# Attention scores as plain float32 products instead of three products of high and low parts

## The chip, the cores and the metric

The kernel runs on one core of a Trainium2 chip. The metric is the device time of one execution in microseconds (us), median of three runs. The engines are named as the profile names them: PE (TensorE: matrix products; PEld its weight loads), DVE (VectorE), ACT (ScalarE), POOL (GpSimd) and SP (which issues most DMAs). Each works through its own queue in order, and they meet through semaphores.

## What is computed

A causal attention is followed by two mixture-of-experts layers. Only the attention is touched by the change:

```python
batch, n_heads, seq, head_dim = (4, 12, 448, 64)
scale = 1.0 / np.sqrt(q.shape[-1])
scores = scale * np.matmul(q, k.transpose(0, 1, 3, 2))
mask = np.triu(np.ones((seq, seq), dtype=bool), k=1)
scores = np.where(mask, -1000000000.0, scores)
scores = scores - np.max(scores, axis=-1, keepdims=True)
attn = np.exp(scores)
attn = attn / (np.sum(attn, axis=-1, keepdims=True) + 1e-09)
return np.matmul(attn, v).astype(np.float32)
```

Its output, 1792 tokens of 768 numbers, goes through a layer with 8 experts (two products with 768x1024 and 1024x768 weights per expert) and then through a second one of the same size.

## The kernel before

**Tiling.** The 48 heads are worked as 24 pairs. The two heads of a pair (e = 0, 1) lie in partitions 0 to 63 and 64 to 127 of one tile `r` that holds keys and queries, transposed, as 2x448 columns of float32. The 448 queries of a head are cut into four chunks of 112; chunk c needs the keys of chunks 0 to c only, 112(c+1) columns. A score tile `sc` is one PSUM bank (128x512 float32), and there are four of them: two chunks of two heads.

**Scores.** `qk(g, c)` makes the scores of pair g and chunk c for both heads. Queries and keys have each been split by `split_pair` into a high part `hi` (type float32r, which PE multiplies in one record) and a low part `lo`; the score is the sum of hi·hi, hi·lo and lo·hi (L423), the two heads alternating, and a last product per head adds the mask (L425, bfloat16, `identb` times `mask`, 1e30 above the diagonal; scores are negated, so the row's minimum is the maximum). `split_pair` runs on POOL two pairs ahead: it scales the queries in place (L386), copies to `hi` (L164, in `pcopy`) and subtracts for `lo` (L167, in `psub`). For the first two pairs it runs on DVE and ACT (L392 to L396).

**Around them.** Per pair and chunk, `rowmax` (L430, DVE) takes the row minimum from PSUM into `nm`, `expo` (L435, ACT) reads the same bank and writes `ex`, which frees the bank. `halves_hi` (ACT, L443) and `halves_lo` (DVE, L448, `al<-ex,ah`) split `ex` in two 16-bit parts that DMAs transpose; `last_chunk` transposes chunk 3 on PE (L457) and splits it (L460, L462). `values` multiplies with the values (L490, L494), `combine` normalises (L501 to L509), `route_t` and `route_l` (L518 to L531) prepare the routing of the first expert layer. `split_v` (POOL, L167, `r<-vr` and `r<-r`) splits the values.

**Order.** All queues are written out by hand in one loop over g (L800): pair g's scores, pair g-1's last chunk, pair g-2's values, pair g-3's routing. In PE's queue an iteration reads: chunks 0 and 1 of pair g; transposes; `values` of head 0; chunks 2 and 3 of pair g; transposes; `values` of head 1; `route_l`. Small routing steps on DVE are dealt out between the others by `tick`.

Of the kernel before, what the change touches and what calls it, by code (L numbers as in the profile page):

```python
# [9 lines left out]
F32 = mybir.dt.float32  # L10
F32R = mybir.dt.float32r
# [5 lines left out]
ALU = mybir.AluOpType  # L17
# [6 lines left out]
P = 128  # L24
B, H, S, HD = 4, 12, 448, 64
CP, NCH = 112, 4
NT, D, F, E = 1792, 768, 1024, 8
# [17 lines left out]
NAH = 2  # L45
NTH = 3
NTP = 2
PLACES = (0, 7, 2, 4, 6, 5, 3, 1)
AHEAD = 2
NONE = 2.0 * E * E + E  # L50
# [5 lines left out]
def attention_two_moe_kernel(  # L56
# [17 lines left out]
    vec, act, pool, pe = nc.vector, nc.scalar, nc.gpsimd, nc.tensor  # L74
# [15 lines left out]
    mask = const.tile([CP, 512], BF16, name="mask")  # L90
# [3 lines left out]
    zero8 = const.tile([P, E], F32, name="zero8")  # L94
    vec.memset(zero8, 0.0)
    st_v, st_x, st_q = ExitStack(), ExitStack(), ExitStack()
    right = lambda st, nm, bufs: st.enter_context(tc.tile_pool(name=nm, bufs=bufs, side="right", reuse_waits="tile"))
# [2 lines left out]
    av_p = right(st_v, "av_p", 1)  # L100
    xb_p = right(st_v, "xb_p", 2)
    at_p = right(st_x, "at_p", 1)
    ld_p = right(st_q, "ld_p", 4)
    raw = right(st_q, "raw", 1)
    ps_s = st_q.enter_context(tc.tile_pool(name="ps_s", bufs=4, space=PSUM, side="right", reuse_waits="tile"))

    his, los = ([raw.tile([P, 2 * S + P - CP], F32R, name=f"{nm}{i}") for i in range(3)] for nm in ("hi", "lo"))
    for t in his + los:
        for k in range(0, P - CP, E):
            vec.tensor_copy(t[:, 2 * S + k : 2 * S + k + E], zero8)  # L110
    identb = const.tile([CP, P], BF16, name="identb")
    vec.tensor_copy(identb, ident[:CP])
    iota_i = const.tile([P, JB * E], I32, name="iota_i")
# [49 lines left out]
    def pcopy(dst, src):  # L163
        pool.tensor_scalar(out=dst, in0=src, scalar1=1.0, scalar2=1.0, op0=ALU.mult, op1=ALU.mult)  # L164

    def psub(dst, a, b):
        pool.tensor_tensor(out=dst, in0=a, in1=b, op=ALU.subtract)  # L167
# [158 lines left out]
    tls = [av_p.tile([P, 2 * ND * CP + 16], F16, name=f"tl{i}") for i in range(NTH)]  # L326
    phs = [av_p.tile([CP, 2 * NCH * CP + 16], F16, name=f"ph{i}") for i in range(NTP)]
    pls = [av_p.tile([CP, 2 * NCH * CP + 16], F16, name=f"pl{i}") for i in range(NTP)]
    for t in ahs + als:
# [38 lines left out]

    NPR = B * H // 2
    PB = H // 2  # L370
    raws, spl, vrs, vss = {}, {}, {}, {}
    def load_pair(g):
        b, i = divmod(g, PB)
        r = ld_p.tile([P, 2, S], F32, tag="r", name=f"r{g}")
# [5 lines left out]
        vrs[g] = av_p.tile([CP, 2, NCH, HD], F32, tag="vr", name=f"vr{g}", bufs=6)  # L380
        nc.sync.dma_start(vrs[g], vh[b, :, 2 * i : 2 * i + 2])

    def split_pair(g, fast=False):
        r = raws.pop(g)
        if not fast:
            pool.tensor_scalar(out=r[:, 1], in0=r[:, 1], scalar1=-0.125, scalar2=1.0, op0=ALU.mult, op1=ALU.mult)  # L386
        hi, lo = his[g % 3], los[g % 3]
        spl[g] = hi[:, :S], lo[:, :S], hi[:, S:], lo[:, S:]
        r = r.rearrange("p k s -> p (k s)")
        hi, lo = hi[:, : 2 * S], lo[:, : 2 * S]  # L390
        if fast:
            vec.tensor_scalar(out=hi[:, S:], in0=r[:, S:], scalar1=-0.125, scalar2=1.0, op0=ALU.mult, op1=ALU.mult)  # L392
            act.copy(hi[:, :S], r[:, :S])
            vec.scalar_tensor_tensor(out=lo[:, S:], in0=r[:, S:], scalar=-0.125, in1=hi[:, S:].bitcast(F32),
                                     op0=ALU.mult, op1=ALU.subtract)
            vec.tensor_sub(lo[:, :S], r[:, :S], hi[:, :S].bitcast(F32))  # L396
        else:
            pcopy(hi, r)
            psub(lo, r, hi.bitcast(F32))

    def split_v(g):
        r0 = vrs.pop(g)
# [7 lines left out]
    boff = [0, 1, 3, 6]  # L410
    scs, nms, avs = {}, {}, {}

    def qk(g, c):

        kh, kl, qh, ql = spl[g]
        n = CP * (c + 1)
        cs = slice(c * CP, (c + 1) * CP)
        for e in range(2):
            scs[2 * g + e, c] = ps_s.tile([P, 512], F32, tag="sc", name=f"sc{2 * g + e}_{c}")
        for st, (a, b) in enumerate(((qh, kh), (qh, kl), (ql, kh))):  # L420
            for e in range(2):
                rs = slice(e * HD, (e + 1) * HD)
                pe.matmul(scs[2 * g + e, c][:, :n], lhsT=a[rs, c * CP : c * CP + P], rhs=b[rs, :n], start=(st == 0), stop=False)  # L423
        for e in range(2):
            pe.matmul(scs[2 * g + e, c][:, cs], lhsT=identb, rhs=mask[:, :CP], start=False, stop=True)  # L425

    def rowmax(h, c):
        if c == 0:
# [246 lines left out]
            load_v(g)  # L675
    load_consts()
    clear_meta()
    split_pair(0, True)
    xbs = {}
    routing = prep_en()  # L680
    for _ in range(8):
# [118 lines left out]
    for g in range(NPR + 3):  # L800
        t, v, r = g - 1, g - 2, g - 3
        if g + 4 < NPR:
            load_pair(g + 4)
        if g + 3 < NPR:
            load_v(g + 3)
        if r == 0:
            drain(routing)
            routing = None
            vec.tensor_scalar_mul(tau_h, tau_t, 0.5)
            vec.reciprocal(tau_r, tau_h)  # L810
            for b in range(B):
                vec.tensor_copy(mts[b][:, :, 3], mod_i[:, b * NCH : (b + 1) * NCH, 0])
        if 0 <= v < NPR and v % PB == 0:
            xbs[v // PB] = xb_p.tile([CP, NCH, D], F32, tag="xb", name=f"xb{v // PB}")
        late = [last_chunk(t, e) if 0 <= t < NPR else iter(()) for e in range(2)]
        if g < NPR:
            for c in range(2):
                qk(g, c)
        tick(True)
        if g < NPR:  # L820
            for c in range(2):
                both(rowmax, g, c)
                if g == c == 0:
                    both(expo, 0, 0, ticks=False)
                    split_pair(1, True)
            for c in range(g == 0, 2):
                both(expo, g, c, ticks=False)
        next(late[0], None)
        next(late[0], None)
        if 0 <= t < NPR:  # L830
            halves_lo(t, (0,))
        next(late[0], None)
        if 0 <= t < NPR:
            halves_lo(t, (1,))
        if g == NPR + 2:
            warm(ps_T, "T", WV)
        if 0 <= r < NPR:
            if r == NPR - 1:
                for c in range(NCH):
                    route_ss(B - 1, c, xbs[B - 1], 2)  # L840
                last_root = route_root(B - 1)
                next(last_root)
            route_t(r, xbs[r // PB])
            if r == NPR - 2:
                for c in range(NCH):
                    route_ss(B - 1, c, xbs[B - 1], 1)
        if g == NPR + 1:
            split_w(1, (4, 5), range(3))
            warm(ps_T, "T", WV)
        if 0 <= v < NPR:  # L850
            values(v, 0)
        if PB <= r < NPR and r % PB < NCH:
            b = r // PB - 1
            c = -1
            for c in ((0,), (1,), (2,), (3,))[r % PB] if b < B - 2 else ((0, 1), (2, 3), (), ())[r % PB]:
                store_x(b, c)
                route_ss(b, c, xbs[b])
            if c == NCH - 1:
                drain(routing or ())
                routing = route1(b)  # L860
        if g < NPR:
            for c in range(2, NCH):
                qk(g, c)
                both(rowmax, g, c)
        next(late[1], None)
        for c in range(2, NCH):
            if g < NPR:
                both(expo, g, c, ticks=False)
            next(late[1], None)
        if 0 <= v < NPR:  # L870
            values(v, 1)
        if 0 <= r < NPR:
            route_l(r)
        if 0 <= v < NPR:
            combine(v, xbs[v // PB])
        if g < NPR:
            halves_hi(g)
        if g + 2 < NPR:
            split_pair(g + 2)
        if g == 0:  # L880
            split_v(0)
        if g + 1 < NPR:
            split_v(g + 1)
        if LEAD <= g <= NPR:
            for c in range(g - LEAD, KD if g == NPR else g - LEAD + 1):
                load_lead(m1, 1, c)
        if g == NPR - 1:
            st_q.close()
            ps_h = left("ps_h", 2, space=PSUM)
            ps_T = left("ps_T", 2, space=PSUM)  # L890
            wh, w1l = left("wh", 1), ()
            w1h = [wh.tile([P, F], F32R, name=f"w1h{c}") for c in range(KD)]
            for k in range(2):
                pcopy(w1h[k], w1r[k])
        if g == NPR:
            split_w(1, (2, 3), ())
            st_x.close()
            wb = left("wb", 1)
            w1l = [wb.tile([P, F], F32R, name=f"w1l{c}") for c in range(KD)]
            w2r = [wb.tile([P, D], F32, name=f"w2r{f}") for f in range(KF)]  # L900
            m1.gather_early((0,), 2 * S)
            load_lead(m1, 2)
        if g == NPR + 2:
            split_w(1, (), range(3, KD))
    drain(routing)
    b = B - 1
# [630 lines left out]
```

## Time and profile before

| | us |
|---|---|
| median of three runs | 921.96 |
| the three runs | 918.61, 923.04, 921.96 |
| the profiled execution, its own time | 910.5 |
| span of its trace | 908.7 |

The profiled execution is a run of its own, 1.2% under the median of the three; between its span and its time lie 1.8 us. Times in the trace count from the span's start. Matmuls overlap, and the end of one is modelled; what one costs in a row of them is read from start to start.

### The profile page before, as it was taken

How to read it: one execution, taken by the hardware profiler on the slowest of the kernel's cores; microseconds unless marked ns; L12 is line 12 of the kernel's file. 1: busy time of each engine (PE TensorE's matmuls, PEld its weight loads, DVE VectorE, ACT ScalarE, POOL GpSimd, SP SyncE). 2: the span in 40 equal slices, each digit the busy share in tenths (PEclk: the TensorE clock that was granted, in tenths of full speed). 3: DMA queues.
4: the chain of work that ended last, by engine and by line, in shares of the span. 5: the costliest groups of instructions: out<-in, count | busy, mean ns of one | idle time of the engine just before them, and what ended most of it. 6: DMA issues, size and time to landing. Idle time of an engine off the chain costs nothing. (4 is left out here: it accounts for less than half of the span.)

```text
span 908.7 us, 21165 instructions
## 1 busy us (share of the span) xinstructions
PE 859.1 (95%) x7010; PEld 753.3 (83%) x7010; DVE 699.3 (77%) x1798; ACT 427.8 (47%) x779; POOL 478.0 (53%) x477
## 2 busy tenths in 40 slices
PE   4999999999789899999999999999999999999995
PEld 3877877877577899998898999888899898898984
DVE  7899999999785766787936884468886678976793
ACT  3676777767434664575525652245112133312323
POOL 7877577875255255454444564431653544544531
PEclk9999999999899999999999999999999999999998
DMA  6799996979717765578515662120281233511110
GB/s 193 161 154 171 203 181 159 210 172 218 241 53 254 278 257 176 203 282 296 193 38 183 201 231 97 53 76 6 57 332 39 67 88 133 185 48 54 54 38 16
DMA packets 114456, 137.46 MB, mean 151 GB/s; under 512 B 78382, under 2 KB 82788, under 8 KB 114289
## 3 DMA queue, kind: packets, MB, share of 16 engines
q1 hardware_dynamic: 101376, 108.76, 44.1%
q0 software_dynamic: 12912, 26.83, 9.4%
q8 instruction: 61, 1.00, 0.5%
q14 instruction: 107, 0.87, 0.3%
HBM read 101.48 MB, written 19.92 MB: 134 GB/s over the span
## 5 line engine op out<-in xcount | busy, mean ns | idle before, releaser
L765 POOL DMA_INDIRECT xg<-x,xi x128 | 137.7, 1076 | 98.3 <-DMA x<-yb,mg 50.8
L974 PE MATMUL h<-w1h,xh 128*128 128x512 f32 x408 | 165.0, 404 | 1.0 <-ACT xh L958 1.0
L976 PE MATMUL h<-w1h,xl 128*128 128x512 f32 x408 | 161.5, 396 | 1.0 <-DVE xl L959 1.0
L975 PE MATMUL h<-w1l,xh 128*128 128x512 f32 x408 | 161.3, 395 | 0.2 <-DVE w1l L715 0.2
L1039 PE MATMUL o<-w2h,hh 128*128 128x384 f32 x528 | 138.3, 343 | 0.2 <-ACT hh L988 0.2
L1039 PE MATMUL o<-w2h,hl 128*128 128x384 f32 x528 | 136.7, 340 | 0.9 <-DVE hl L989 0.9
L1039 PE MATMUL o<-w2l,hh 128*128 128x384 f32 x528 | 136.0, 339 | 0.1
L1016 DVE STREAM_TRANSPOSE hs<-h 32x256 f32<-32x256 f32 x240 | 107.0, 446 | 14.3 <-PE h L976 9.0
L435 ACT ACTIVATE ex<-sc,nm 112x112 f32<-112x112 f32 (+1 forms) x192 | 83.8, 503 | 62.2 <-DVE nm L430 60.9
L1039 PEld LDWEIGHTS o<-w2h,hl 128*128 128x128 f32 x528 | 96.4, 190 | 1.2 <-DVE hl L989 1.2
L1039 PEld LDWEIGHTS o<-w2l,hh 128*128 128x128 f32 x528 | 96.1, 189 | 0.7 <-DVEq L1330 0.4
L1039 PEld LDWEIGHTS o<-w2h,hh 128*128 128x128 f32 x528 | 94.8, 190 | 1.8 <-ACT hh L988 0.4
L976 PEld LDWEIGHTS h<-w1h,xl 128*128 128x128 f32 x408 | 77.3, 190 | 19.6 <-DVE xl L959 2.0
L1022 ACT ACTIVATE hh<-hs 128x512 fp32r<-128x512 f32 x30 | 18.4, 631 | 158.1 <-PE o L1039 88.6
L974 PEld LDWEIGHTS h<-w1h,xh 128*128 128x128 f32 x408 | 77.5, 190 | 16.6 <-ACT xh L958 1.1
L975 PEld LDWEIGHTS h<-w1l,xh 128*128 128x128 f32 x408 | 77.5, 190 | 16.2 <-DVE w1l L715 1.0
L715 DVE TENSOR_TENSOR w1l<-w1r,w1h 128x1024 fp32r<-128x1024 f32 x66 | 76.5, 1221 | 8.3 <-ACT w1h L713 7.5
L430 DVE TENSOR_REDUCE nm<-sc 112x1 f32<-112x112 f32 (+1 forms) x192 | 75.6, 439 | 6.1 <-PE sc L425 5.0
L715 DVE TENSOR_TENSOR w2l<-w2r,w2h 128x768 fp32r<-128x768 f32 x78 | 68.8, 953 | 8.2 <-ACT w2h L713 6.9
L713 ACT CAST w1h<-w1r 128x1024 fp32r<-128x1024 f32 x64 | 62.4, 1046 | 8.4 <-PE h L976 5.2
L947 DVE STREAM_TRANSPOSE xr<-xg 128x768 f32<-128x768 f32 x31 | 50.4, 1625 | 18.8 <-DMA xg<-x,xi 14.9
L713 ACT CAST w2h<-w2r 128x768 fp32r<-128x768 f32 x78 | 58.5, 849 | 0.6 <-ACTq L1421 0.6
(327 smaller groups left out, 1932.7 us busy)
## 6 DMA issues: line engine op xcount, KB each, us to landing
w1r<-in_w1a SPq DMA_DIRECT2D x48, 512.0 KB, 6.8
w2r<-in_w2a SPq DMA_DIRECT2D x64, 384.0 KB, 6.2
r<-in_kqP SPq DMA_DIRECT2D x24, 448.0 KB, 4.3
w1r<-in_w1b SPq DMA_DIRECT2D x18, 512.0 KB, 6.5
w2r<-in_w2b SPq DMA_DIRECT2D x24, 384.0 KB, 6.4
vr<-in_vh SPq DMA_DIRECT2D x24, 224.0 KB, 4.4
x<-xb SPq DMA_DIRECT2D x16, 336.0 KB, 4.3
xg<-x,xi POOLq DMA_INDIRECT x128, 3.3
```

The costliest lines, as they stand in the source:

```text
L430: vec.tensor_reduce(out=nms[h][:, c : c + 1], in_=scs[h, c][:CP, : CP * (c + 1)], axis=AX.X, op=ALU.min)
L435: act.activation(dst, scs.pop((h, c))[:CP, :n], AF.Exp, bias=nms[h][:, c : c + 1], scale=-1.0)
L713: act.copy(hi[k], r[k])
L715: vec.tensor_sub(lo[k], r[k], hi[k].bitcast(F32))
L765: pool.indirect_dma_start(out=xgs[j % 3][:, q * (D // Q) : (q + 1) * (D // Q)], out_offset=None, in_=quarters, in_offset=IND(ap=xi[:, q : ...
L947: vec.transpose(xr.rearrange("p k (q r) -> p q k r", q=Q), xgs[j % 3].rearrange("p (q r k) -> p q k r", q=Q, k=KD))
L974: pe.matmul(hps, lhsT=xh[:, c], rhs=w1h[c][:, ns], start=(c == 0), stop=False)
L975: pe.matmul(hps, lhsT=xh[:, c], rhs=w1l[c][:, ns], start=False, stop=False)
L976: pe.matmul(hps, lhsT=xl[:, c], rhs=w1h[c][:, ns], start=False, stop=(c == KD - 1))
L1016: vec.transpose(hr[cols, :, rows], hps[rows, q * 256 : (q + 1) * 256].rearrange("p (c k) -> p k c", c=QR))
L1022: act.activation(hh[k], part, AF.Relu)
L1039: pe.matmul(ops[:, n, :384], lhsT=h[f // KH][:, f % KH], rhs=w[f][:, n * 384 : (n + 1) * 384], start=(f == 0 and st == 0), stop=(f == KF - ...
```

## The change

`split_pair`, the tiles `hi` and `lo` and the 12 copies that clear their ends are gone. `scale_pair` scales the queries in place (DVE for the first two pairs, POOL afterwards), and the scores are one product per head and chunk of the raw float32 keys and the scaled float32 queries. `qk` now takes two chunks at once: four mask products come first and open the four sums, then four score products close them. The weights of a score product have 112 columns rather than 128. The load tiles `r` are six instead of four, since PE reads them now.

```diff
-    ld_p = right(st_q, "ld_p", 4)
-    raw = right(st_q, "raw", 1)
+    ld_p = right(st_q, "ld_p", NLD)
...
-    def split_pair(g, fast=False):
-        r = raws.pop(g)
-        if not fast:
-            pool.tensor_scalar(out=r[:, 1], in0=r[:, 1], scalar1=-0.125, scalar2=1.0, op0=ALU.mult, op1=ALU.mult)
...
-        else:
-            pcopy(hi, r)
-            psub(lo, r, hi.bitcast(F32))
+    def scale_pair(g, eng):
+        q = raws[g][:, 1]
+        eng.tensor_scalar(out=q, in0=q, scalar1=-0.125, scalar2=1.0, op0=ALU.mult, op1=ALU.mult)
...
-    def qk(g, c):
...
-        for st, (a, b) in enumerate(((qh, kh), (qh, kl), (ql, kh))):
-            for e in range(2):
-                rs = slice(e * HD, (e + 1) * HD)
-                pe.matmul(scs[2 * g + e, c][:, :n], lhsT=a[rs, c * CP : c * CP + P], rhs=b[rs, :n], start=(st == 0), stop=False)
-        for e in range(2):
-            pe.matmul(scs[2 * g + e, c][:, cs], lhsT=identb, rhs=mask[:, :CP], start=False, stop=True)
+    def qk(g, cs):
+
+        r = raws[g] if cs[-1] < NCH - 1 else raws.pop(g)
+        for c in cs:
+            for e in range(2):
+                sc = scs[2 * g + e, c] = ps_s.tile([P, 512], F32, tag="sc", name=f"sc{2 * g + e}_{c}")
+                pe.matmul(sc[:, c * CP : (c + 1) * CP], lhsT=identb, rhs=mask[:, :CP], start=True, stop=False,
+                          skip_group_check=True)
+        for c in cs:
+            n = CP * (c + 1)
             for e in range(2):
                 rs = slice(e * HD, (e + 1) * HD)
+                pe.matmul(scs[2 * g + e, c][:CP, :n], lhsT=r[rs, 1, c * CP : n], rhs=r[rs, 0, :n], start=False, stop=True,
+                          skip_group_check=True)
...
-    split_pair(0, True)
+    scale_pair(0, vec)
...
-            for c in range(2):
-                qk(g, c)
+            qk(g, (0, 1))
...
-                    split_pair(1, True)
+                    scale_pair(1, vec)
...
+            qk(g, (2, 3))
             for c in range(2, NCH):
-                qk(g, c)
                 both(rowmax, g, c)
...
-            split_pair(g + 2)
+            scale_pair(g + 2, pool)
```

In PE's queue before, this is chunk 0 of the third pair (`hi_108` and `lo_111` hold its parts, `sc_0_534` and `sc_0_535` are the score tiles of its two heads); chunk 1 follows in the same form:

```order
L423 MATMUL sc_0_534<-hi_108 128x112
L423 MATMUL sc_0_535<-hi_108 128x112
L423 MATMUL sc_0_534<-lo_111,hi_108 128x112
L423 MATMUL sc_0_535<-lo_111,hi_108 128x112
L423 MATMUL sc_0_534<-hi_108,lo_111 128x112
L423 MATMUL sc_0_535<-hi_108,lo_111 128x112
L425 LDWEIGHTS identb
L425 MATMUL sc_0_534<-mask,identb 128x112
L425 LDWEIGHTS identb
L425 MATMUL sc_0_535<-mask,identb 128x112
```

The same place of the changed kernel holds chunks 0 and 1 (`r_265` is the pair's tile of keys and queries):

```order
L401 LDWEIGHTS identb
L401 MATMUL sc_0_471<-mask,identb 128x112
L401 LDWEIGHTS identb
L401 MATMUL sc_0_473<-mask,identb 128x112
L401 LDWEIGHTS identb
L401 MATMUL sc_1_475<-mask,identb 128x112
L401 LDWEIGHTS identb
L401 MATMUL sc_1_477<-mask,identb 128x112
L407 MATMUL sc_0_471<-r_265 112x112
L407 MATMUL sc_0_473<-r_265 112x112
L407 MATMUL sc_1_475<-r_265 112x224
L407 MATMUL sc_1_477<-r_265 112x224
```

Sixteen products of two chunks have become eight; the mask products of both chunks moved ahead of all score products, and the two heads no longer alternate product by product over three rounds: each head's product is one instruction.

In POOL's queue before, one iteration of the loop in mid-attention (`r_529` is the tile of the pair two ahead, `vr_531` the values of the pair one ahead):

```order
L386 TENSOR_SCALAR r_529<-r_529 128x448
L164 TENSOR_SCALAR hi_106<-r_529 128x896
L167 TENSOR_TENSOR lo_109<-r_529,hi_106 128x896
L167 TENSOR_TENSOR r_257<-vr_531 112x8x64
L167 TENSOR_TENSOR r_1145<-r_257 112x512
```

The changed kernel has there, for this and the iteration before it:

```order
L381 TENSOR_SCALAR r_386<-r_386 128x448
L163 TENSOR_TENSOR r_235<-vr_388 112x8x64
L163 TENSOR_TENSOR r_839<-r_235 112x512
L381 TENSOR_SCALAR r_466<-r_466 128x448
L163 TENSOR_TENSOR r_236<-vr_468 112x8x64
L163 TENSOR_TENSOR r_1028<-r_236 112x512
```

Two of five operations per pair have left POOL's queue, the copy to `hi` and the subtraction for `lo`; the scaling and the splitting of the values stay in their order.

## Rows read from the trace of the kernel before

**Rows 1.** The page: share of the span by engine.

```profile
PE 859.1 (95%) x7010; PEld 753.3 (83%) x7010; DVE 699.3 (77%) x1798; ACT 427.8 (47%) x779; POOL 478.0 (53%) x477
```

**Rows 2.** Windows: stretch, length, busy of PE, PEld, DVE, ACT, POOL; granted clock, DMA, GB/s.

```profile
63.50:140.80 77.30, 73.59 (x1339) 60.76 (x1338) 73.91 (x173) 55.86 (x126) 55.15 (x47) 1.00 1.01 184
140.80:150.90 10.10, 8.77 (x154) 7.06 (x153) 10.03 (x30) 7.79 (x18) 5.11 (x5) 1.00 0.57 127
```

**Rows 3.** Timeline of PE: first score products of pairs 3, 12 and 23 (start, us).

```profile
37.47 0.32 PE L423 MATMUL sc<-hi 64*128 64x112 f32 x2
...
114.08 0.32 PE L423 MATMUL sc<-hi 64*128 64x112 f32 x2
...
213.46 0.32 PE L423 MATMUL sc<-hi 64*128 64x112 f32 x2
```

**Rows 4.** Timeline of PE: chunks 0 and 1 of pair 11 (start, us).

```profile
105.77 0.36 PE L531 MATMUL lg<-xTl,enT 128*16 128x448 f32 x1
106.06 0.32 PE L423 MATMUL sc<-hi 64*128 64x112 f32 x2
...
106.54 0.27 PE L425 MATMUL sc<-mask,identb 112*128 112x112 bf16 x2
106.74 0.37 PE L423 MATMUL sc<-hi 64*128 64x224 f32 x2
...
107.37 0.55 PE L457 MATMUL tb<-ident,ex 112*112 112x112 f32 x4
```

**Rows 5.** Timeline of PE: chunks 2 and 3 of pair 10.

```profile
101.66 0.20 PE L490 MATMUL av<-r,pl 112*128 112x65 bf16 x1
...
102.96 0.37 PE L423 MATMUL sc<-lo,hi 64*128 64x448 f32 x2
103.16 0.37 PE L423 MATMUL sc<-hi,lo 64*128 64x448 f32 x2
...
103.57 0.55 PE L457 MATMUL tb<-ident,ex 112*112 112x112 f32 x4
103.96 0.17 PE L493 MATMUL av<-r,th 112*128 112x1 bf16 x1
```

**Rows 6.** Timeline of PE's weight loads for chunk 3 of pair 10.

```profile
102.65 0.19 PEld L423 LDWEIGHTS sc<-hi 64*128 64x128 f32 x2
102.76 0.19 PEld L423 LDWEIGHTS sc<-lo,hi 64*128 64x128 f32 x2
```

**Rows 7.** One line, L1090: products with both operands plain float32; min/median/max ns.

```profile
L1090 PE MATMUL pl<-wg,yT x216: 171/256/293, 284.5 to 628.9; 128*128 128x8 f32 x108
```

**Rows 8.** Timeline of PE: chunk 2 of the first pair; one head, then both.

```profile
11.67 0.48 PE L423 MATMUL sc<-lo,hi 64*128 64x336 f32 x1
...
11.67 0.72 PE L423 MATMUL sc<-lo,hi 64*128 64x336 f32 x2
11.95 0.72 PE L423 MATMUL sc<-hi,lo 64*128 64x336 f32 x2
```

**Rows 9.** Groups by form, DVE, 37.5 to 213.5: busy us, mean ns.

```profile
L448 DVE SCALAR_TENSOR_TENSOR al<-ex,ah 112x672 f16<-112x672 f32 x40 | 42.4, 1060 | 0.0
```

**Rows 10.** One line, L448: min/median/max ns over the whole run.

```profile
L448 DVE SCALAR_TENSOR_TENSOR al<-ex,ah x48: 836/849/1577, 23.6 to 226.2; 112x672 f16<-112x672 f32 x48
```

**Rows 11.** Timeline of DVE in the first pair.

```profile
12.45 2.51 DVE L396 TENSOR_TENSOR lo<-r,hi 128x448 fp32r<-128x448 f32 x1
14.88 1.50 DVE L430 TENSOR_REDUCE nm<-sc 112x1 f32<-112x224 f32 x4
```

**Rows 12.** Timeline of PE in the first pair: what chunk 3 waits for.

```profile
15.79 1.08 PE L423 MATMUL sc<-hi 64*128 64x448 f32 x2 [2.82 <-ACT ex L435]
16.33 0.91 PE L423 MATMUL sc<-lo,hi 64*128 64x448 f32 x2
16.70 0.91 PE L423 MATMUL sc<-hi,lo 64*128 64x448 f32 x2
```

**Rows 13.** Timeline of ACT: exponentials of chunk 3, pair 10, both heads.

```profile
104.60 1.15 ACT L435 ACTIVATE ex<-sc,nm 112x448 f32<-112x448 f32 x2
```

More of the change, by code (lines that the diff above doesn't have):

```diff
@@ L47 @@
 NTP = 2
+NLD = 6
 PLACES = (0, 7, 2, 4, 6, 5, 3, 1)
@@ L102, in attention_two_moe_kernel @@
     at_p = right(st_x, "at_p", 1)
-    ld_p = right(st_q, "ld_p", 4)
-    raw = right(st_q, "raw", 1)
+    ld_p = right(st_q, "ld_p", NLD)
     ps_s = st_q.enter_context(tc.tile_pool(name="ps_s", bufs=4, space=PSUM, side="right", reuse_waits="tile"))
[L107 to L110, printed above, removed]
     identb = const.tile([CP, P], BF16, name="identb")
@@ L370, in attention_two_moe_kernel @@
     PB = H // 2
-    raws, spl, vrs, vss = {}, {}, {}, {}
+    raws, vrs, vss = {}, {}, {}
     def load_pair(g):
@@ L381, in load_v @@
         nc.sync.dma_start(vrs[g], vh[b, :, 2 * i : 2 * i + 2])
-    def split_pair(g, fast=False):
-        r = raws.pop(g)
-        if not fast:
-            pool.tensor_scalar(out=r[:, 1], in0=r[:, 1], scalar1=-0.125, scalar2=1.0, op0=ALU.mult, op1=ALU.mult)
[L387 to L396, printed above, removed]
-        else:
-            pcopy(hi, r)
-            psub(lo, r, hi.bitcast(F32))
+    def scale_pair(g, eng):
+        q = raws[g][:, 1]
+        eng.tensor_scalar(out=q, in0=q, scalar1=-0.125, scalar2=1.0, op0=ALU.mult, op1=ALU.mult)
     def split_v(g):
@@ L411, in attention_two_moe_kernel @@
     scs, nms, avs = {}, {}, {}
-    def qk(g, c):
-        kh, kl, qh, ql = spl[g]
-        n = CP * (c + 1)
-        cs = slice(c * CP, (c + 1) * CP)
-        for e in range(2):
-            scs[2 * g + e, c] = ps_s.tile([P, 512], F32, tag="sc", name=f"sc{2 * g + e}_{c}")
-        for st, (a, b) in enumerate(((qh, kh), (qh, kl), (ql, kh))):
+    def qk(g, cs):
[7 more added lines that the diff above has]
+            n = CP * (c + 1)
             for e in range(2):
                 rs = slice(e * HD, (e + 1) * HD)
-                pe.matmul(scs[2 * g + e, c][:, :n], lhsT=a[rs, c * CP : c * CP + P], rhs=b[rs, :n], start=(st == 0), stop=False)
-        for e in range(2):
-            pe.matmul(scs[2 * g + e, c][:, cs], lhsT=identb, rhs=mask[:, :CP], start=False, stop=True)
+                pe.matmul(scs[2 * g + e, c][:CP, :n], lhsT=r[rs, 1, c * CP : n], rhs=r[rs, 0, :n], start=False, stop=True,
+                          skip_group_check=True)
     def rowmax(h, c):
```

## The prediction

> **What bounds the kernel now.** On the page [rows 1] PE is busy 95% of the span. The change touches the attention alone, so I read that stage: the windows by pair, then PE's timeline inside a pair. From pair 3 at 37.47 to pair 23 at 213.46 lie 20 pairs in 176 us [rows 3], 8.80 each; pair 11, from 106.06 to 114.08, takes 8.02 [rows 3, 4]. The nine pairs of the first window [rows 2] have PE busy 73.6 of 77.3 and DVE 73.9, which is 8.2 of DVE per pair; the single pair of the second window takes 10.1, and there DVE is busy 10.0 and PE 8.8. So two engines are near their limit: PE sets the quick pairs (8.0), DVE the long ones, where the routing steps come on top. About half of the 20 pairs are near 8.0, so the others average about 9.6; this halving is an estimate from the mean of 8.80. ACT and POOL have room in both windows.
>
> **PE, what leaves.** Scores of chunks 0 and 1 reach from the end of L531's columns to the transposes at 107.37 [rows 4]. A 448-column record costs 0.20 from start to start (102.96 to 103.16 [rows 5]), so L531 streams until 105.97 and the block costs 1.40. Chunks 2 and 3 reach from 101.69 (the last value product starts at 101.66 and needs 0.03) to 103.57 [rows 5]: 1.88. Together 3.28 per pair, all of which the change replaces.
>
> **PE, what comes.** Four small parts of each block have rows. Two mask products and the change to score products last from 106.54 to 106.74 [rows 4]: at 0.45 ns a column (below) 112 columns are 0.05, so the turn takes about 0.10. The first weights take 0.11 (102.65 to 102.76 [rows 6]). The turn back costs another 0.10. A block therefore has 0.20 + 0.10 + 0.10 + 0.10 = 0.50 beside its score columns.
>
> The score columns are the unknown. The trace has plain float32 products in one place, L1090: six products in each of 18 blocks, 108, and 216 records [rows 7], so each product is two records. With 8 columns they don't show what a column costs. Bounds: the float32r records run 448 columns in 0.20, 0.45 ns a column [rows 5]; the transposes at L457, whose operands are plain float32, go four in 0.39 (103.57 to 103.96 [rows 5]), 0.098 for 112 columns, 0.87 ns each. I take 0.87, since the transposes have the operand type of the new products: a record then costs 0.10, 0.20, 0.29 and 0.39 for chunks 0 to 3. The Trainium skill, in "FP8 and Floating Point Precision" (TensorE Precision Notes), gives true FP32 four passes through the array; on two records that is two passes each, dearer than the three records that go, and a rule against this change. By it the sum would be the one with 0.87; a single pass per record would be the one with 0.45.
>
> The order decides the rest. Before, the heads alternate and run side by side, since each has its own half of the rows. Now head 0's two records come before head 1's, so head 0's second runs beside head 1's first, and head 1's second beside head 0's first of the next chunk. That shifted records do overlap is seen in the first pair: two products of 336 columns, one for each head, span 0.72 where one lasts 0.48, so head 1 starts 0.24 late, yet the next product of head 0 starts at 0.28 after its last (11.67 to 11.95 [rows 8]), which is one record's columns at the halved pace of that stretch (448 columns take 0.37 there, 16.33 to 16.70 [rows 12], against 0.20 later). Two chunks with four records each make five steps: 0.10 + 0.10 + 3 x 0.20 = 0.80, and 2 x 0.29 + 3 x 0.39 = 1.75. With 0.50 each the blocks cost 1.30 and 2.25, together 3.55: **+0.27 per pair** on PE.
>
> **POOL and DVE.** POOL loses two of its five operations a pair. PE waits for none of them in the quick pairs, so that alone is worth nothing; but DVE's L448 takes 0.85 in the middle and up to 1.58 [rows 10], and 1.06 in the mean of the stage [rows 9], while POOL works on the same memory. Two per pair: if all excess goes, 2 x 0.21 = 0.43 of DVE per pair. Short routing steps seem to suffer the same way; I put them at 0.3 per long pair, an estimate between nothing and the 0.7 by which a single L448 is stretched. If `split_v` keeps colliding, the relief is nothing.
>
> **Start.** DVE makes `lo` for pair 1 before the row minima of pair 0's chunk 1: L396 alone takes 2.51, the minima follow at 14.88, and chunk 3's products stand 2.82 at 15.79 for the exponential behind them [rows 11, 12]. Instead DVE has one scaling of 448 columns. Of the 2.8 I count 2: PE goes at half its later pace there, so dearer columns cost double (+0.5 in each of the first pairs), and the masks now wait for the last bank before any product of the block can start. Net of the three first pairs: -1. The twelve clearing copies ahead of that lie before DVE's wait for POOL's constants and count nothing; if they were on the path, about 1 us more.
>
> **No cost.** The masks wait for the bank of chunk 3, head 1: its exponential ends at 104.60 + 1.15 = 105.75 [rows 13], and the masks could start at 105.97: covered by 0.2, thinly. The scaling on POOL runs two pairs ahead. Six load tiles: PE frees a tile two iterations before its next load, so SP's queue doesn't wait.
>
> **Sum.** Ten quick pairs, PE-bound: +0.27 each, +2.7. Ten long pairs, DVE-bound: -0.43 - 0.3, together -7.3. Start -1. Total -5.6; I say **-5**. On the profiled 910.5 that is 905.5; the median stands 11.5 above that execution, and I expect the same of the new one: **917**. With no DVE relief the sum is +2 (924); with twice the routing relief and the whole 2 of the start it is -10 (912). With 2 more for the halving on either side the forecast's own range is 910 to 926.
>
> **Rivals.**
>
> Heads in turn (slower): if records of a plain float32 product don't run beside those of the other head, a pair has eight steps: 4 x 0.10 + 4 x 0.20 = 1.20 and 4 x 0.29 + 4 x 0.39 = 2.72, 1.37 more than above, 1.64 more than before. All pairs then take about 9.65, where the long ones take 9.6 already: 20 x 9.65 - 176 = +17; double in the first three pairs, some +6; start -1. 944. For it: the heads no longer alternate. Against: rows 8. It decides from about 0.5 us per pair on.
>
> Cheap columns (faster): with 0.45 ns the five steps of a block are 0.10 to 0.11 each, bounded by the weight loads, 0.53, and 2 x 0.15 + 3 x 0.20 = 0.90; with 0.50 each 2.43, 0.85 less than before. DVE at 8.2 less 0.4 to 0.7 allows about as much: 20 x -0.85, less 3 at the start, gives 902. For it: nothing but the missing row; against it the transposes.
>
> Masks held: if the exponential of chunk 3 slips by more than 0.2 behind PE, both chunks wait where before only chunk 1 did; up to 0.5 per pair, +12: 929. For it: the thin cover, and DVE's lateness in the long pairs; against: dearer score blocks move PE's arrival later too.
>
> Exposed weights: the second record of a product loads weights for the rows whose columns are still streaming. If that load waited, four of five steps would show 0.11 each, 0.88 per pair: 20 x 9.17 - 176 = +7, +3 in the first pairs, start -1: 931. The load of the second round starts at 102.76 and its product at 102.96 [rows 6, 5], while the first round's columns run: the load is hidden. The Trainium skill ("TensorE: Matmul & The Clock Gate", The mechanism) has loads overlap running matmuls only in another row group, which is this rival; the trace disagrees.
>
> **Chances.** The forecast 0.67, heads in turn 0.17, cheap columns 0.07, masks held 0.06, exposed weights 0.03. The bound of what can be told apart is 0.5%, 4.6 us: below 917.4 is faster, above 926.6 slower. The forecast splits 0.37 faster, 0.27 same, 0.03 slower; with the others: faster 0.44, same 0.28, slower 0.28. The range reaches from 904 to 940: it holds the forecast, both small slow cases, the lower part of heads in turn and the upper edge of cheap columns.
>
> **What would show it.** In the changed trace: twice as many score records as instructions, 448 columns at about 0.39 from start to start; head 1's first record starting with head 0's second (apart by a few ns; in turn, if a whole record apart); blocks of about 1.30 and 2.25; L448 near 0.85 throughout; quick pairs near 8.3 and long ones nearer 9. I'm wrong if blocks exceed 5 us together, if PE waits for `ex` ahead of the masks in most pairs, or if L448 keeps its 1.06.

## The result and the profile after

| | us | 95% interval |
|---|---|---|
| before, median of 4 runs beside it | 920.29 | |
| after, median of 4 runs (907.46 to 912.15) | 909.6 | |
| ratio | 0.9898 | 0.9857 to 0.9938 |
| profiled execution after, own time; span | 908.99; 907.3 | |

The changed kernel is about 1% faster. The profiled execution of before (910.5) was a low one among its runs (916.77 to 923.04), so the two traces are only 1.4 us apart in span, and what each part is worth has to come from the experiments. The traces say what happens inside a pair.

Page of the kernel after, share of the span by engine (answers to [rows 1]):

```profile
PE 848.7 (94%) x6818; PEld 729.4 (80%) x6818; DVE 678.2 (75%) x1782; ACT 427.1 (47%) x777; POOL 399.0 (44%) x433
```

POOL has lost 79 us and DVE 21. Windows of the kernel after with the columns of [rows 2]: the nine pairs from the seventh (pair 6) on, then pairs 15 and 16 alone:

```profile
61.31:136.15 74.84, 70.86 (x1267) 54.78 (x1265) 68.04 (x177) 56.31 (x127) 28.03 (x30) 1.00 1.02 185
136.15:144.62 8.47, 7.93 (x147) 6.18 (x145) 8.16 (x30) 7.41 (x18) 1.77 (x4) 1.00 0.76 165
144.62:155.68 11.06, 9.55 (x142) 6.86 (x141) 8.26 (x26) 7.64 (x17) 8.81 (x12) 0.85 0.96 210
```

DVE is busy 7.56 us per pair in the first window, where it had 8.2. Pair 16, in the third, takes 11.06 us with fewer PE and DVE instructions than pair 15 (142 against 147, 26 against 30), at a granted clock of 0.85.

PE's timeline after, chunks 2 and 3 of pair 10, then chunks 0 and 1 of pair 12 (answers to [rows 4, 5]; the first windows are cut between the records, so a row counts those that start close together):

```profile
97.52 0.36 PE L401 MATMUL sc<-mask,identb 112*128 112x112 bf16 x4
97.81 0.54 PE L407 MATMUL sc<-r 64*112 64x336 f32 x2
98.19 0.82 PE L407 MATMUL sc<-r 64*112 64x336 f32 x4
98.47 0.92 PE L407 MATMUL sc<-r 64*112 64x448 f32 x4
98.84 0.54 PE L407 MATMUL sc<-r 64*112 64x448 f32 x2
99.32 0.31 PE L440 MATMUL tb<-ident,ex 112*112 112x112 f32 x1
...
109.84 0.37 PE L514 MATMUL lg<-xTl,enT 128*16 128x448 f32 x1
110.05 0.37 PE L401 MATMUL sc<-mask,identb 112*128 112x112 bf16 x4
110.35 0.83 PE L407 MATMUL sc<-r 64*112 64x112 f32 x8
111.12 0.41 PE L440 MATMUL tb<-ident,ex 112*112 112x112 f32 x2
```

Two instructions of 336 columns and two of 448 make eight records, but they begin at only four times: 97.81, 98.19, 98.47, 98.84, two records each, one of either head. A 336-column step takes 0.28 (98.19 to 98.47), a 448-column step 0.37 (98.47 to 98.84), 0.84 ns a column. The block lasts from 97.52 to 99.32, 1.80; the one of chunks 0 and 1 from the end of L514's columns at 110.04 (0.20 after its start) to 111.12, 1.07. Together 2.87 per pair, where before had 3.28. Blocks of chunks 0 and 1 take 1.07 to 1.11 in 14 of the 20 pairs from pair 4 on; in the others a mask product starts late and they take 1.18 to 1.84.

One line of the kernel after, `al<-ex,ah` on DVE (now L431, min/median/max ns; answers to [rows 10]):

```profile
L431 DVE SCALAR_TENSOR_TENSOR al<-ex,ah x48: 824/848/1090, 19.4 to 225.1; 112x672 f16<-112x672 f32 x48
```

Groups by form after, 34.5 to 213.5 (answers to [rows 9]):

```profile
L431 DVE SCALAR_TENSOR_TENSOR al<-ex,ah 112x672 f16<-112x672 f32 x40 | 34.1, 852 | 0.0
```

The stretched ones (up to 1577 before) are gone. The short routing steps show it more sharply. One of them, 32 elements with two inputs in SBUF, is this line of the kernel before (min/median/max ns):

```profile
L219 DVE TENSOR_TENSOR am_ohr<-am_ohr,iota8m x4: 184/608/2089, 136.0 to 250.3; 112x32 f32<-112x32 f32 x4
```

The same line of the kernel after:

```profile
L215 DVE TENSOR_TENSOR am_ohr<-am_ohr,iota8m x4: 181/184/191, 131.9 to 246.9; 112x32 f32<-112x32 f32 x4
```

A step of 0.18 us took up to 2.09 before. The timelines of DVE and POOL before show that instance and what stands beside it:

```profile
136.00 2.09 DVE L219 TENSOR_TENSOR am_ohr<-am_ohr,iota8m 112x32 f32<-112x32 f32 x1
...
135.36 2.68 POOL L167 TENSOR_TENSOR lo<-r,hi 128x896 fp32r<-128x896 f32 x1
```

It ends at 138.09, 0.05 after POOL's subtraction.

PE's timeline, the first score products of pairs 3 and 23 after (answers to [rows 3]):

```profile
34.53 0.83 PE L407 MATMUL sc<-r 64*112 64x112 f32 x8
...
213.51 0.35 PE L407 MATMUL sc<-r 64*112 64x112 f32 x2
```

Pair 3 begins 2.9 us earlier than before; the 20 pairs behind it take 179.0 in this execution against 176.0. Who waited for whom after, from 34.5 to 213.5 (total us, times, longest), PE and then DVE:

```profile
PE av L473 <- DMA tl<-al: 7.3, 8, 1.7
PE av L473 <- issue: 2.5, 5, 0.6
PE sc L401 <- ACT ex L418: 1.2, 4, 0.3
...
DVE nm L413 <- PE sc L407: 11.8, 9, 3.4
```

Before, from 37.5 to 213.5, PE waited 3.1 us for `tl<-al`, "issue" was not among its longer waits, and DVE waited 1.6 us for scores. Windows of the kernel after, parts of two of the three pairs that take 11 us or more there:

```profile
148.00:156.00 8.00, 7.27 (x102) 5.00 (x104) 5.28 (x12) 4.72 (x10) 6.13 (x8) 0.79 0.83 203
204.00:212.00 8.00, 6.46 (x58) 4.18 (x58) 3.73 (x7) 3.32 (x9) 7.38 (x8) 0.57 1.06 204
```

PE stood in pieces of 0.4 to 1.1 us, in the first case ahead of the stretch (two, from 147 to 149.3), in the second at its start (four, from 203.2 to 206.2, two of them before the clock falls at 205); the granted clock is 0.79 and 0.57, that is, it stands at the lower of its two levels, 1.2 GHz, for much of the stretch, and PE needs longer for the work that the others wait for: the eight score records of chunks 2 and 3 span 1.57 us at 97.81 and 2.96 at 207.05.

### The profile page after: what moved, and what is told of

Same layout as the page of the kernel before. It is cut to its first block, busy times and chain, and to the rows that moved or that the text cites. A ratio compares the mean times of both kernels' runs of the same rounds, so it can differ in the third digit from the quotient of the medians.

```text
span 907.3 us, 20634 instructions
## 1 busy us (share of the span) xinstructions
PE 848.7 (94%) x6818; PEld 729.4 (80%) x6818; DVE 678.2 (75%) x1782; ACT 427.1 (47%) x777; POOL 399.0 (44%) x433
## 5 line engine op out<-in xcount | busy, mean ns | idle before, releaser
L748 POOL DMA_INDIRECT xg<-x,xi x128 | 134.4, 1050 | 101.2 <-DMA x<-yb,mg 47.7
L407 PE MATMUL sc<-r 64*112 64x112 f32 (+3 forms) x384 | 64.5, 458 | 3.9 <-DVE rt_ren L175 3.9
```

Of the source, the lines that this page charges most:

```text
L407: pe.matmul(scs[2 * g + e, c][:CP, :n], lhsT=r[rs, 1, c * CP : n], rhs=r[rs, 0, :n], start=False, stop=True, skip_group_check=True)
L748: pool.indirect_dma_start(out=xgs[j % 3][:, q * (D // Q) : (q + 1) * (D // Q)], out_offset=None, in_=quarters, in_offset=IND(ap=xi[:, q : ...
```

## The experiments

Each ratio is to runs of the kernel before made beside it; e1 to e4 were measured together, e5 to e8, and e9 to e12.

| | median us | ratio | 95% interval |
|---|---|---|---|
| e1_one_chunk | 906.76 | 0.9871 | 0.9825 to 0.9918 |
| e2_parts_masks_first | 914.97 | 0.9983 | 0.9957 to 1.001 |
| e3_pool_kept | 926.2 | 1.0087 | 1.0052 to 1.0121 |
| e4_parts_once | 908.82 | 0.991 | 0.9879 to 0.9941 |
| e5_heads_apart | 914.55 | 0.9957 | 0.9932 to 0.9983 |
| e6_pool_in_step | 919.64 | 1.0009 | 0.9978 to 1.004 |
| e7_masks_twice | 908.62 | 0.988 | 0.9841 to 0.9919 |
| e8_after_again | 911.3 | 0.991 | 0.9878 to 0.9941 |
| e9_chunk3_first | 908.14 | 0.9858 | 0.9823 to 0.9893 |
| e10_one_and_chunk3 | 910.0 | 0.9887 | 0.9858 to 0.9917 |
| e11_scale_on_act | 914.54 | 0.9943 | 0.9922 to 0.9965 |
| e12_start_kept | 915.48 | 0.9936 | 0.9908 to 0.9965 |

### POOL's work, with either kind of product

The two halves of the change were separated. In e4 the kernel before keeps its score products, and POOL stops making parts after pair 2; later pairs read the old parts again:

```diff
-        else:
+        elif g < 3:
             pcopy(hi, r)
             psub(lo, r, hi.bitcast(F32))
```

> The kernel before, in which POOL makes high and low parts for pair 2 alone and later pairs read the parts of pairs 0 to 2 again (the queries are still scaled; the copy and the subtraction are left out, so the scores are those of other pairs): PE's queue of before with the POOL load of the changed kernel. Theory A: DVE's 0.43 per pair and the short routing steps are relieved, PE stays at 8.0 in quick pairs: 914 to 917, ratio 0.993 to 0.997. Rival D: no change, 0.999 to 1.002. Rival E (POOL's load is the whole gain): ratio 0.986 to 0.991.

0.991: nearly the whole gain, with the old products and the old start. Rival E had it (0.986 to 0.991); theory A, with about half of it, had not, though the interval reaches into its range. Windows of e4, about from pair 3 to 23:

```profile
37.70:209.00 171.30, 164.07 (x2989) 135.56 (x2984) 158.22 (x428) 131.22 (x291) 65.60 (x80) 1.00 0.99 184
```

Groups by form of DVE in e4, the same stretch:

```profile
L448 DVE SCALAR_TENSOR_TENSOR al<-ex,ah 112x672 f16<-112x672 f32 x40 | 36.4, 911 | 0.0
```

From the first score product of pair 3 at 37.76 to that of pair 23 at 208.60 the 20 pairs take 170.8 us with the old products, 5.2 less than before.

In e3 the changed kernel lets POOL go on copying and subtracting, into tiles that nothing reads:

```diff
         eng.tensor_scalar(out=q, in0=q, scalar1=-0.125, scalar2=1.0, op0=ALU.mult, op1=ALU.mult)
+        if eng is pool:
+            r = raws[g].rearrange("p k s -> p (k s)")
+            pcopy(his[g % 2], r)
+            psub(los[g % 2], r, his[g % 2].bitcast(F32))
```

> The changed kernel, with POOL still making a high and a low part of every pair from the third on, into tiles that nobody reads: the same PE queue as the changed kernel, the same POOL load as before. Theory A: L448's counterpart on DVE goes back to about 1.06 in the mean and the relief of 0.4 to 0.7 per pair is lost: 914 to 918, ratio 0.993 to 0.998. Rival D (POOL's load is free, PE's blocks are the whole gain): as the changed kernel, ratio 0.987 to 0.992.

1.0087, slower than the kernel before, which neither of the two expected. The timelines of DVE and POOL in e3 show the place:

```profile
79.52 2.71 DVE L437 SCALAR_TENSOR_TENSOR al<-ex,ah 112x672 f16<-112x672 f32 x1
...
77.78 1.57 POOL L162 TENSOR_SCALAR hi<-r 128x896 fp32r<-128x896 f32 x1
79.43 2.08 POOL L165 TENSOR_TENSOR lo<-r,hi 128x896 fp32r<-128x896 f32 x1
```

POOL's subtraction starts 0.09 before `al<-ex,ah`, which then lasts 2.71: POOL's 2.08 and most of its own 0.85. Seven pairs in a row, from 47.4 to 114.7, take 9.6 us each, and in six of them the second `al<-ex,ah` lasts 2.7. In the kernel before, POOL's copy had waited for PE's last score product of an older pair, which put the subtraction elsewhere in the pair. POOL's waits before, 37.5 to 213.5:

```profile
POOL hi L164 <- PE sc L425: 16.7, 8, 3.5
```

So e6 repeats e3 with that wait: three tiles of each part, and PE reads 8 columns of each behind chunk 3, which makes its block of chunks 2 and 3 2.04 instead of 1.80.

```diff
+        if c == NCH - 1 and g > 1:
+            for k, t in enumerate((his[g % 3], los[g % 3])):
+                pe.matmul(sc[:, S + 8 * k : S + 8 * k + 8], lhsT=t[:, :P], rhs=t[:, :8], start=True, stop=True,
+                          skip_group_check=True)
```

> The changed kernel, but POOL still makes the high and low parts, as in the kernel before, into three tiles each, and TensorE reads 8 columns of either at the end of chunk 3 (two small products into unused columns), so that POOL has to wait for it as it did before. No result is used. Theory place (what made POOL's kept work slower than the kernel before was where it fell: its 2.1 us subtraction on the second `al<-ex,ah` of a pair, 2.7 us): in step again, `al<-ex,ah` has about 1.06 in the mean, no row of 2.7, and the time is that of the kernel before less the start and a little of the score blocks: 0.992 to 1.0. Rival load (the same POOL work costs the same wherever it falls): `al<-ex,ah` stays at 1.3 or more, 1.005 to 1.012.

1.0009: no longer slower than before, and not faster. The theory of the place had 0.992 to 1.0, just missed; the rival's 1.005 to 1.012 is out. Two forms of DVE in e6, in the attention:

```profile
L442 DVE SCALAR_TENSOR_TENSOR al<-ex,ah 112x672 f16<-112x672 f32 x40 | 37.8, 944 | 0.0
...
L215 DVE TENSOR_TENSOR am_ohr<-r1lgr,am_mxr 112x32 f32<-112x32 f32 x2 | 2.9, 1440 | 0.0
```

No instance of 2.7 is left (2.14 is the longest), but a step such as the second, 0.18 us in the kernel after, still pays for POOL.

The four cells: parts made, split products 1; parts made, plain products 1.0009 (1.0087 out of step, e3); no parts, split products 0.991; no parts, plain products 0.990. The gain goes with POOL's two operations and not with the products. With the new products the two operations are worth as much as with the old: e6 takes 919.64 beside 911.3 of e8, the changed kernel measured with it, 8.3 us. The Trainium skill, "SBUF — State Buffer" (section "SBUF: two separate sides"), says that VectorE and GpSimd share one pair of ports, which a VectorE operation with two SBUF inputs or a GpSimd operation that reads SBUF, whichever starts first, holds whole while the other stands fully blocked; the 2.71 beside 2.08 agrees.

### The order of masks and heads

e2 gives the kernel before the new order alone: four masks first, then the split products of two chunks.

```diff
-        for e in range(2):
-            pe.matmul(scs[2 * g + e, c][:, cs], lhsT=identb, rhs=mask[:, :CP], start=False, stop=True)
...
+        for c in cs:
+            for e in range(2):
+                sc = scs[2 * g + e, c] = ps_s.tile([P, 512], F32, tag="sc", name=f"sc{2 * g + e}_{c}")
+                pe.matmul(sc[:, c * CP : (c + 1) * CP], lhsT=identb, rhs=mask[:, :CP], start=True, stop=False,
+                          skip_group_check=True)
```

> The kernel before (high and low parts, three products), with only the order changed: four mask products of two chunks first, then their score products. Theory A: blocks of PE shrink by one turn each way, about 1.40 to 1.16 and 1.88 to 1.56, -0.56 per pair, more than the changed kernel's, but DVE still carries 8.2 per pair, so the long pairs stay and the quick ones gain little: ratio 0.993 to 1.000. Rival C (the order of the masks is the whole gain): ratio 0.985 to 0.992, as the changed kernel.

0.9983 (0.9957 to 1.001): no change, as theory A had it, though the block of chunks 2 and 3 takes 1.58 instead of 1.88. e1 takes the order back out of the changed kernel, so that each chunk's masks stand before its own products:

```diff
-            qk(g, (0, 1))
+            for c in range(2):
+                qk(g, (c,))
...
-            qk(g, (2, 3))
             for c in range(2, NCH):
+                qk(g, (c,))
                 both(rowmax, g, c)
```

> The changed kernel, but each chunk's two mask products stand directly ahead of its own two score products, as separate blocks, instead of four masks and then four score products of two chunks. Theory A (the gain has three parts: shorter score blocks on PE, DVE freed from POOL's two operations, an earlier start; grouping two chunks saves one turn each way per block): two more turns each way and two more first weight loads per pair, 2 x 0.3 = +0.6 on PE per pair over the changed kernel, so quick pairs stay near the old 8.0 and only DVE's relief and the start are left: 915 to 919 where the kernel before has 920.3, ratio 0.994 to 0.999. Rival B (grouping is worth nothing because the masks then wait for the bank of chunk 3): as the changed kernel or faster, ratio 0.985 to 0.992.

PE's timeline in e1, chunks 2 and 3:

```profile
106.35 0.26 PE L401 MATMUL sc<-mask,identb 112*128 112x112 bf16 x2
106.54 0.54 PE L407 MATMUL sc<-r 64*112 64x336 f32 x2
106.92 0.45 PE L407 MATMUL sc<-r 64*112 64x336 f32 x2
107.30 0.27 PE L401 MATMUL sc<-mask,identb 112*128 112x112 bf16 x2
107.50 0.63 PE L407 MATMUL sc<-r 64*112 64x448 f32 x2
107.97 0.54 PE L407 MATMUL sc<-r 64*112 64x448 f32 x2
108.44 0.40 PE L440 MATMUL tb<-ident,ex 112*112 112x112 f32 x2
```

The block takes 2.09 instead of 1.80: a second turn to masks and back, and a second first weight load (the steps before a turn take 0.38 and 0.47, of which 0.28 and 0.38 are columns). The block of chunks 0 and 1 takes 1.36 where the kernel after has 1.07. Yet the ratio is 0.9871, so what the order saves on PE does not show in the time. Theory A's 0.994 to 0.999 is out, and rival B's number came true. Of its reason a part is seen: in the kernel after, the blocks that masks hold up exceed 1.07 and 1.80 by 3.3 us in all between pairs 3 and 23, outside the stretches of low clock; in e1 such blocks are rare.

e5 keeps the order of the masks and writes all of head 0's products of a block before head 1's:

```diff
-        for c in cs:
-            n = CP * (c + 1)
-            for e in range(2):
+        for e in range(2):
+            for c in cs:
+                n = CP * (c + 1)
```

> The changed kernel, but inside a block head 0's products of both chunks come first and then head 1's; masks, tiles and the number of products are unchanged. Theory own queues (each half of the rows works through its own products, so the order in which the heads are written is indifferent): the records of both heads still stand side by side, the blocks keep 1.2 and 1.8 us, 0.986 to 0.994 of the kernel before. Rival next in line (only the product next in the queue can start beside a running one): head 0's four records run alone but for the last, so chunks 2 and 3 need 2 x 0.28 + 2 x 0.38 + 0.28 + 2 x 0.38 = 2.35 where the trace after has 1.31, chunks 0 and 1 1.03 for 0.56; +1.5 us per pair on TensorE, of which the pairs that VectorE sets swallow about half: 1.005 to 1.03.

PE's timeline in e5, chunks 2 and 3:

```profile
99.74 0.55 PE L407 MATMUL sc<-r 64*112 64x336 f32 x2
100.11 0.83 PE L407 MATMUL sc<-r 64*112 64x336 f32 x4
100.39 0.93 PE L407 MATMUL sc<-r 64*112 64x448 f32 x4
100.77 0.55 PE L407 MATMUL sc<-r 64*112 64x448 f32 x2
101.25 0.31 PE L440 MATMUL tb<-ident,ex 112*112 112x112 f32 x1
```

The same four steps, with the second head's record starting 0.01 behind the first's: own queues holds for the records, and next in line, which was the prediction's picture, falls. The time fits neither: 0.9957 lies between the two ranges, and the median is 3.2 us above that of e8 beside it (914.55 and 911.3). The block of chunks 2 and 3 is no longer; that of chunks 0 and 1 takes 1.2 to 1.3 in most pairs, since its fourth mask product starts 0.17 to 0.29 behind the third instead of 0.05. As e7 below adds more than that without loss, the cause of the 3 us stays open.

### Is PE's time worth anything?

e7 writes every mask product of the changed kernel twice:

```diff
+                for _ in range(2):
-                pe.matmul(sc[:, c * CP : (c + 1) * CP], lhsT=identb, rhs=mask[:, :CP], start=True, stop=False,
-                          skip_group_check=True)
+                    pe.matmul(sc[:, c * CP : (c + 1) * CP], lhsT=identb, rhs=mask[:, :CP], start=True, stop=False,
+                              skip_group_check=True)
```

> The changed kernel with every mask product written twice (the second overwrites the first with the same numbers): eight more products of 0.05 to 0.06 us per pair, about 0.45 us more on TensorE and nothing else. Theory given back (the score blocks are shorter by 0.28 us, but TensorE then waits for the DMA behind VectorE's `al<-ex,ah`, and the granted clock falls after such waits; VectorE sets the mean): quick pairs near 8.3, fewer stretches with a clock under 0.9 than in the changed kernel, time as the changed kernel in the same call, within 0.4%. Rival TensorE (its work in the quick pairs is the time): ten quick pairs x 0.45 + three first pairs x 0.8 = +7 us, 0.8% above the changed kernel in the same call.

e8 is the changed kernel itself:

> The changed kernel once more, to stand beside the three others on the same chip: 0.986 to 0.994 of the kernel before, with two to four stretches of low clock in the second half of the attention if these belong to the kernel, at other places or none if they are chance.

PE's timeline in e7: masks 0.49 instead of 0.29 ahead of the first product, 0.20 more in each block.

```profile
99.09 0.56 PE L402 MATMUL sc<-mask,identb 112*128 112x112 bf16 x8
99.58 1.57 PE L408 MATMUL sc<-r 64*112 64x336 f32 x8
101.08 0.59 PE L441 MATMUL tb<-ident,ex 112*112 112x112 f32 x4
```

That is 0.4 per pair, 8 us over 20 pairs, and the ratio is 0.988 beside e8's 0.991. Even half of it, 4 us or 0.44%, is not there: theory given back has the time, rival TensorE is out. The shortest pairs do get longer with PE's work. PE's timelines of the kernel after and of e1, first score products of two pairs in a row:

```profile
155.68 0.35 PE L407 MATMUL sc<-r 64*112 64x112 f32 x2
...
163.41 0.35 PE L407 MATMUL sc<-r 64*112 64x112 f32 x2
```

```profile
155.06 0.35 PE L407 MATMUL sc<-r 64*112 64x112 f32 x2
...
163.32 0.45 PE L407 MATMUL sc<-r 64*112 64x112 f32 x4
```

The pair takes 7.7 after and 8.25 in e1; the shortest of before take 8.0 and those of e7 8.05. In this order the blocks of a pair are 2.87, 3.45, 3.28 and 3.27. So PE sets the shortest pairs, as the prediction read, but the sum of all pairs does not follow them.

Theory given back expected fewer stretches of low clock. Windows of e7, the two stretches shown for the kernel after:

```profile
148.00:156.00 8.00, 6.89 (x131) 5.55 (x131) 6.71 (x18) 5.71 (x13) 7.42 (x9) 1.00 0.98 199
204.00:212.00 8.00, 7.13 (x78) 4.94 (x78) 3.40 (x7) 3.49 (x9) 6.62 (x8) 0.57 0.86 221
```

One is gone, one stays. In e8 the first stands elsewhere (56 to 64, 0.79) and the second at 204 to 212 again (0.57). So the late stretch comes back in all three profiles, and the earlier one moves from run to run; that filling PE's time removes it is not shown by one profile.

### What is left to gain

e9 lets `values` begin with chunk 3, whose parts need no DMA; e10 does so on top of e1:

```diff
-        for c in range(NCH):
+        for c in (NCH - 1, *range(NCH - 1)):
             k = c if e == 0 else NCH + (c - 1) % NCH
```

> The changed kernel, but `values` starts with chunk 3, whose parts come from TensorE's own transposes, and goes on with chunks 0 to 2, whose parts come by DMA; the same 100 products per pair in another order. Theory late DMA (TensorE's 7 us of waits for `tl<-al` and the falls of the granted clock behind them are what is left of the attention's loss): the twenty products of chunk 3 give the DMA 0.6 us more, the waits fall below 4 us, and the time lies 2 to 5 us under the changed kernel (0.984 to 0.988 of the kernel before). Rival VectorE sets the mean: TensorE waits at another place instead, 0.988 to 0.993.

> The same order of `values` together with the masks of one chunk directly before that chunk's products. If the two add up, 0.981 to 0.986 of the kernel before; if the time hangs on VectorE and POOL alone, as the changed kernel, 0.987 to 0.993.

e9 has the lowest ratio of all, 0.9858, and PE's waits for `tl<-al` fall from 7.6 us in e8 to 4.3; but its interval overlaps that of the changed kernel, and e10 at 0.9887 gives no sign that the two add up. Neither is shown to beat it.

e11 takes the scaling from POOL too:

```diff
-            scale_pair(g + 2, pool)
+            act.activation(raws[g + 2][:, 1], raws[g + 2][:, 1], AF.Copy, scale=-0.125)
```

> The changed kernel, but ScalarE scales the queries from the third pair on and POOL has only the splitting of the values left. Theory relief goes on (each POOL operation taken away speeds VectorE): 0.5 to 0.8 us of POOL less per pair, 2 to 3 us less time, 0.984 to 0.989. Rival relief used up (`al<-ex,ah` stands at 0.85 already, its shortest): no change against the changed kernel, 0.988 to 0.993, or slower by up to 2 us where ScalarE's 0.55 us delay the high parts of the next pair.

0.9943: not faster, and above what either theory expected, with an interval that still overlaps that of the changed kernel. Pair 3 begins at 36.72, 2.2 later than after; that the scaling stands in ScalarE's way there is likely, not shown. Beyond that PE waits 3.4 us, 12 times, for the exponential ahead of the masks. How much each costs was not separated.

e12 restores DVE's and ACT's work for the first two pairs, into unread tiles:

```diff
+        if eng is vec:
+            k, hi, lo = raws[g][:, 0], his[g], los[g]
+            act.copy(hi[:, :S], k)
+            vec.scalar_tensor_tensor(out=lo[:, S:], in0=q, scalar=-0.125, in1=k, op0=ALU.mult, op1=ALU.subtract)
+            vec.tensor_sub(lo[:, :S], k, hi[:, :S].bitcast(F32))
```

> The changed kernel, but for the first two pairs VectorE and ScalarE also make parts that nothing reads, with the operations of the kernel before at the same places. If the start is worth what the traces show at pair 3 (34.5 after, 37.5 before), pair 3 begins near 37 again and the time is 2 to 3 us above the changed kernel: 0.992 to 0.995. If that lead is given back later, pair 3 begins near 37 but the time is that of the changed kernel: 0.988 to 0.992.

PE's timeline in e12, first score product of pair 3:

```profile
40.24 0.83 PE L414 MATMUL sc<-r 64*112 64x112 f32 x8
```

5.7 later than in the kernel after, and 2.8 later than before, so e12 takes back more than the lighter start. Two reasons can be read there: a 448-column step costs 0.75 in the second pair (25.88 to 26.63) instead of 0.37 later, and in the first pair the masks of chunk 3 wait until 14.69 for their bank, with the products of chunk 2 behind them, which were under way at 11.67 before [rows 8]. How much each costs was not separated. The ratio is 0.9936 against 0.9898 and 0.991, 2 to 4 us, with intervals that overlap; what the start is worth is not resolved.

## Why the prediction was right, and where not

It forecast 917, faster than before, because POOL's two operations leave DVE free; measured 909.6, faster, inside the range of 904 to 940 and 0.4 below the forecast's own 910 to 926. The direction came from the term that was right. The size was half of what was measured: the term for PE, +2.7, was wrong, and the one for the start may have been too small. The step from a profiled execution to the median was also off: after, the profiled execution (908.99) lies 0.6 under the median and not 11.5; it does no harm, since 917 is the old median less 5.

**POOL and DVE: right, and the size too.** 0.43 per pair on `al<-ex,ah` was forecast; the mean went from 1060 to 852, two per pair, 0.42. The whole relief was put at -7.3; e4 gives 0.9% of 916.64, -8 (5 to 11 by its interval), and e6 beside e8 gives 8.3 with the new products. DVE's busy time in the 20 pairs fell from 168.8 (before, 37.5 to 213.5) to 155.8 (after, 34.5 to 213.5), 0.65 per pair, of which `al<-ex,ah` is 0.42. The rest is mostly the short routing steps, which were under-sized: 3 us over ten long pairs were forecast from the 0.7 by which one `al<-ex,ah` is stretched, but a step of 0.18 can be held for 2.09, most of a POOL operation of 2.68. The sentence that without relief the sum is +2 (0.2%) stands beside e6's +0.1%, by luck: its +2.7 for PE was wrong, as told below. What was not seen is that the collision depends on where POOL's operation falls, by as much as the whole gain (e3 against e6, 0.8%).

**What PE's columns cost: right.** 0.87 ns was taken, 0.84 measured; two records for each product, 448 columns at 0.37. The Trainium skill, "FP8 and Floating Point Precision" (TensorE Precision Notes), has four passes for true FP32; two records at about twice the 0.45 ns of a float32r record, taken as one pass, agree. Masks and turn took 0.29 (forecast 0.30), the first weights 0.09 (0.10), the turn back 0.10 (0.10).

**The step that failed: "The order decides the rest", the five steps.** It had head 1's first record wait until head 0's second. The trace has both heads' first records together, then both second ones, four steps, and e5 shows that the written order does not change which records run together. Blocks are 1.07 and 1.80 where 1.30 and 2.25 stood, -0.41 per pair in place of +0.27. [Rows 8] had been read as staggering; a head that starts late and then works through its own queue gives the same rows.

**The second failure: PE's change was counted into the total.** "Ten quick pairs, PE-bound" made +2.7 of it (seven of the 20 pairs of before take 8.0, not ten). With the true blocks the same step would have made -4.1. The shortest pairs did go from 8.0 to 7.7, but neither sum is in the time: e1 adds 0.58 to the blocks and e7 0.4, without any loss, and e6 gains nothing from blocks that are shorter by 0.17. PE busy 95% of a window did not make it the bound of the whole: in the trace after, PE's waits for `tl<-al` have grown from 3.1 to 7.3 us and DVE's for scores from 1.6 to 11.8, and in the two stretches shown the granted clock is low. That these take back what the short pairs gain fits the numbers; no run shows it by itself.

**Start: open.** -1 net was forecast; the trace has pair 3 2.9 earlier, and e12 points to some 3 at the end. Then the terms would be 0 for PE, -8 and -3, together -11, where the medians have -10.7. But the repeat e8 has -7.7 beside its own runs of before (919.0), which -8 alone gives, and e6 has the lighter start too and gains nothing. So the sum that fits is no proof of the start's 3.

**No cost: nearly right.** PE waits 1.2 us in all for the exponential ahead of masks, 4 times; by the blocks' length held masks cost the 3.3 us named under e1. **Rivals.** Heads in turn, exposed weights and cheap columns are each refuted by the four steps of 0.28 and 0.37; masks held, which had +12, by the 3.3.

## What to carry to other kernels

When a change speeds one engine and quiets another, run the two halves apart: here the arithmetic that the change was about did nothing that the time shows, and two operations that left POOL gave nearly all of the gain. An operation on POOL is priced by what it overlaps on DVE, so moving or freeing it can cost as much as it saves; look at what pins it in the pair. Before crediting work taken off an engine that is 95% busy, add the same amount to it and see whether the time moves.

## What was not expected of the hardware

A plain float32 product is two records, and those of the two row halves start about 0.01 us apart or less, whichever order the instructions stand in (e5): a record of head 1 starts before records of head 0 that were queued ahead of it, so PE's queue, said at the start to be worked in order, is so only within a half. A DVE operation of 0.85 us lasted 2.71 beside a POOL operation of 2.08. In the changed kernel PE stands four times for 0.4 to 0.6 us between products of `values`, from 203.2 to 206.2, on "issue", with nothing in the profile that it waits for; from 203 to 206 the DMA share is 1.30. The clock falls at 205, between the second and the third. What PE waits for there is open.
